# One of the first mixer's four weight sums made as a DRAM table, its column tiles paired across halves

## The chip, the cores and the metric

The kernel runs on one core of one Trainium2 chip. The metric is the device time of one execution in microseconds (us): the median of three runs, with the lowest and the highest beside it. A profile of one execution lies beside the runs; its numbers (span, busy times, waits, the start of an instruction) belong to that execution.

## The reference

Sequence length S = 2048, width D = 1024, hidden width F = 3584, bf16 in and out, batch 1. A linear attention block with a residual is followed by a mixer along the sequence with a residual:

```python
def _A_ref(x, wqkv, wo):
    qkv = (lambda x, *d: x.transpose(*d))((x @ wqkv).reshape(B, S, 3, H, Dh), 2, 0, 3, 1, 4)
    q, k, v = qkv[0], qkv[1], qkv[2]
    phi = lambda t: jnp.where(t > 0, t + 1, jnp.exp(t)) + 1e-6
    pq, pk = phi(q), phi(k)
    kv = jnp.einsum("bhsd,bhse->bhde", pk, v)
    ...
    return (lambda x, *d: x.transpose(*d))(o, 0, 2, 1, 3).reshape(B, S, D) @ wo
def _B_ref(x, w1, b1, w2, b2):
    h = _layernorm(x, axis=-1)
    u = jnp.einsum("bsd,sf->bdf", h, w1) + b1
    u = _gelu(u)
    y = jnp.einsum("bdf,fs->bds", u, w2) + b2
    return (lambda x, *d: x.transpose(*d))(y, 0, 2, 1)
x = A_x
h = x + _A_ref(_layernorm(x, axis=-1), A_wqkv, A_wo)
h2 = h + _B_ref(_layernorm(h, axis=-1), B_w1, B_b1, B_w2, B_b2)
```

The first mixer (`Mixer1`) is the product of w1, transposed, with the normalized h: F rows by D columns, summed over S. The second (`Mixer2`) multiplies with w2 and goes back to S rows.

## The kernel before

**Stages.** By the profile's times: layernorm of x and the products for k, v and q up to about 160 us; the output projection, with the residual and the two layernorms behind it folded into one, from about 168 to 225 us; the first mixer from 225 to 382 us; the second to the end.

**Products with seven multiplications.** Nearly all products use Strassen's scheme in Winograd's form: the operands are cut into two by two blocks, and seven products of sums of blocks replace eight. The stationary operand's blocks are called a11, a12, a21, a22, and its four sums are numbered by the product that they serve: sum 5 is a21 + a22, sum 6 is sum 5 - a11, sum 7 is a11 - a21, sum 3 is a12 - sum 6. In the first mixer the two halves of the contraction are the even and the odd row tiles of w1 (tiles of 128 rows), and the two halves of the output rows are two neighbouring column tiles of w1: tiles 2p and 2p + 1 for product p.

**Quads.** Two such products form a quad, which reads one w1 tile of 512 columns (`load_w1(u, part)`, in two or four parts). Four of the seven multiplications of the two (numbers 1, 5, 2 and 3) are done in common, once more by the seven-fold scheme (`Inner`: seven times four matmuls of 256 columns), the other three (4, 6, 7) as 48 matmuls of 512 columns in the gaps. `Quad.asums(m)` makes sum m for both products of a quad in one DVE instruction of 128x2048 elements, in a tile of the pool `sa`, which has four buffers for the first mixer and hands them out in turn. There are seven quads, and so seven such instructions per sum. The first quad's sums are made ahead of time, during the output projection, by the generator `first_sums` (line 1772).

**The output loop** (lines 1823 to 1864) runs over the 16 row tiles i in an order of its own. For each it holds, in program order: PE's matmuls (`out_mm`), the denominators of the attention (`den`), the mean of tile i - 1 on DVE (`h_mean`), the normalization of tile i - 3 on DVE, the evacuation on ACT (`out_evac`), the variance of tile i - 2 by a squaring on ACT (`h_var`, which needs that tile's mean), the scaling of the queries on DVE (`scale_q`), the spreading of the reciprocals to the partitions by SP's transfers (`den_spread`), and at i = 1, 2, 3, 5 and 6 the next step of `first_sums`. For the first nine tiles the residual x is added by an accumulating transfer that POOL issues (line 1716); for the others it is copied to the accumulator before the matmuls (`seed`), from tiles that SP loads.

**Order.** `pin` keeps an instruction in program order among the pinned ones of its engine or queue; the names `hv`, `ht`, `hs` and `hd` pin everything on DVE, PE, ACT and SP. In the output loop nearly everything is pinned. Waits for data are put in by the framework, for DRAM tiles too. A queue such as SP's issues in order: a transfer that has to wait holds up those behind it.

**The first stage.** Row tiles of x are normalized in turn (`ln_stats`, `ln_finish`) and transposed by a DMA that SP issues (line 980), each followed on SP by the load of a later row tile; `x_sums` on DVE reads the transposed tiles. The loop over q (line 1462) runs a `KRun` and a `VRun` for each pair of row tiles.

**What the steps touch.** `load_w1` (147), `load_w2` (163), `Product7.__init__` (327), `Mixer1` (434: the view of the w1 tile, the bias column `ft`), `Mixer2` (469), `Quad.asums` (604), `Quad.run_first` (756), `Quad.run1` with `starting` (798), the loop over q (1462), `out_evac` (1701) and `first_sums` (1772).

Of the kernel before, what the change touches and what calls it, by code (L numbers as in the profile page):

```python
# [10 lines left out]
P = 128  # L11
F32 = mybir.dt.float32
BF16 = mybir.dt.bfloat16
FP16 = mybir.dt.float16
ACT = mybir.ActivationFunctionType
ALU = mybir.AluOpType
# [18 lines left out]
def kernel(  # L35
# [12 lines left out]
    nc = tc.nc  # L48
    x = A_x.flatten_outer_dims()
    o_dram = out.flatten_outer_dims()  # L50
    S, D = x.shape
    F = B_w1.shape[1]
# [94 lines left out]
    def load_w1(u, part, hold=lambda ins: ins, parts=2):  # L147
        if part == 0:
            w1_tiles[u] = w_tile(wpool, WLEN)[:, 0:NS * CW].rearrange("p (k f) -> p k f", f=CW)
        k = slice(part * NS // parts, (part + 1) * NS // parts)  # L150
        hold(nc.sync.dma_start(
            w1_tiles[u][:, k, :],
            B_w1[:, u * CW:(u + 1) * CW].rearrange("(k p) f -> p k f", p=P)[:, k, :],
        ))

    WH = NFP * 2 * P
# [6 lines left out]
    def load_w2(p, second, q=nc.sync, ks=slice(0, NFP)):  # L163
        q.dma_start(
            (odd[p] if second else even[p % 2])[:, ks, :],
            B_w2[:, p * 2 * P:(p + 1) * 2 * P].rearrange("(k two p) s -> p k two s", two=2, p=P)[:, ks, second, :],
        )

    spans = (slice(0, NFP // 2), slice(NFP // 2, NFP))

# [28 lines left out]
        for part in phi_parts(dst, src, n, pool):  # L199
            part()  # L200

    dram = ctx.enter_context(tc.tile_pool(name="dram", bufs=1, space=bass.MemoryType.DRAM))
    sactx = ctx.enter_context(ExitStack())
    mctx = ctx.enter_context(ExitStack())

# [4 lines left out]
    hmov = {}  # L210
# [113 lines left out]
    class Product7:  # L324
        first = 0

        def __init__(self, p, w, nk, mov):
            self.p, self.nk, self.mov = p, nk, mov
            (self.a11, self.a21), (self.a12, self.a22) = [[v[:, :, h * P:(h + 1) * P] for h in range(2)] for v in w]
            self.lhs = {1: self.a11, 2: self.a12, 4: self.a22}  # L330

        def prefetch(self):
# [101 lines left out]
    class Mixer1(Product7):  # L434
        first = NSP // 4

        def __init__(self, p):
            c = (p % 2) * 2 * P
            w = w1_tiles[p // 2][:, :, c:c + 2 * P].rearrange("p (k two) f -> p k two f", two=2)
            super().__init__(p, (w[:, :, 0, :], w[:, :, 1, :]), NSP, hmov)  # L440

        def evac(self, fh, dh, ps, a=0, b=CW):
            ft = 2 * self.p + fh
            act.activation(
                (gE if fh == 0 else gO)[:, self.p, dh * CW + a:dh * CW + b],
                ps[:, a:b], ACT.Gelu_apprx_tanh, bias=b1_sb[:, ft:ft + 1], scale=1.0,
            )
# [20 lines left out]

    class Mixer2(Product7):
        def __init__(self, p):  # L470
            super().__init__(p, (even[p % 2], odd[p]), NFP, gmov)
            self.hr = {}

        def asum(self, m, home=None):
# [57 lines left out]
    class Quad:  # L532
# [71 lines left out]
        def asums(self, m):  # L604
            if not isinstance(self.sts[0], Mixer1):
                for st in self.sts:
                    st.asum(m)
                return
            v = w1_tiles[self.sts[0].p // 2].rearrange("p (k two) (s h f) -> p k two s h f", two=2, s=2, h=2)
            a11, a12, a21, a22 = (v[:, :, k, :, h, :] for h in range(2) for k in range(2))  # L610
            a, b, op = {
                5: (a21, a22, ALU.add),
                6: (self.S.get(5), a11, ALU.subtract),
                7: (a11, a21, ALU.subtract),
                3: (a12, self.S.get(6), ALU.subtract),
            }[m]
            t = self.S[m] = pools["sa"].tile([P, NSP, 2, P], FP16, tag="sa", name="sa")[:]
            for s, st in enumerate(self.sts):
                st.lhs[m] = t[:, :, s, :]
            return dve.tensor_tensor(t, a, b, op)  # L620

        def inner(self, m):
            mov, sink, sink_sum = {
# [132 lines left out]
        def run_first(self, nxt, before_inner, before_second):  # L756
            sts = self.sts
            for st in sts:
                st.p1()
            share(sts)  # L760
            for st in sts:
                st.p2()
            before_inner(slice(0, 2))
            self.in5.mov = self.mov5
            self.interleave(self.in5, self.steps(*[st.p6 for st in sts]))
            before_inner(slice(2, 4))
            nxt.begin1()
            self.base3()
            for i, st in enumerate(sts):
                st.apart = 1  # L770
                st.p7()
                before_second(slice(2 * i, 2 * i + 2))
            sts[0].p3()
            sts[1].p3_mm()
            self.late.append(sts[1].p3_evac)
            return sts, nxt
# [21 lines left out]
        def run1(self, pend, nxt, on_p4, third_sums=None):  # L798
            sts = self.sts
            s4, s6, s7 = self.steps(*[st.p4 for st in pend]), self.steps(*[st.p6 for st in sts]), self.steps(*[st.p7_fill for st in sts])  # L800
            c6, c7 = 3 * len(s6) // 4, len(s7) // 2

            def starting():
                self.in1.sums(slice(2, 4))
                self.asums(5)
                self.in5 = Inner(sts, 5, self.mov5, "i5", self.sink5, self.sum5)
                self.in5.sums(slice(0, 2))
                self.asums(6)
                self.t1 = self.base("t1a")
                for s, st in enumerate(sts):  # L810
                    st.begin(self.t1[:, s, :])

            def gelu(s, dh, t):
                return lambda: sts[s].evac(0, dh, t[:, s, :])

            def before_gelu():
                if third_sums is not None:
                    third_sums(slice(3, 4))
                gelu(0, 0, self.t1)()

            def gelu_late(*args):
                return lambda: self.late.insert(0, gelu(*args))

            self.in1.behind = self.late
            self.interleave(
                self.in1, s4, {"b": starting, "7": lambda: self.in5.sums(slice(2, 4))}, (("b", None), ("7", None))
            )
            self.asums(7)
            in2 = Inner2(sts, 2, self.mov2, "i1", self.add_to(self.t1), None)
            in2.sums()  # L830
            on_p4()
            nxt = nxt()
            share(sts)
            if third_sums is not None:
                third_sums(slice(0, 3))
            self.interleave(self.in5, s6[:c6], flush=(("b", None), ("7", None), ("end", None)), first=1)
            sts[0].finish()
            self.asums(3)
            self.base3()
            in3 = Inner2(sts, 3, self.mov3, "i5", self.add_to(self.t3), None)  # L840
            in3.sums()
            sts[0].with_shared(sts[0].base3, sts[0].B)
            self.interleave(
                in2, s6[c6:] + s7[:c7], {"third": before_gelu, "end": gelu_late(1, 0, self.t1)}, (("7", None),)
            )
            sts[1].with_shared(sts[1].base3, sts[1].B)
            if nxt is not None:
                nxt.begin1()
            self.interleave(in3, s7[c7:], {
                "third": gelu(0, 1, self.t3), "end": gelu_late(1, 1, self.t3),  # L850
            }, (("b", 1), ("c", None)))
            return sts, nxt
# [13 lines left out]
    with ExitStack() as actx:  # L866
# [33 lines left out]
        with ExitStack() as a1:  # L900
# [561 lines left out]
            for q in range(2, NVP):  # L1462
# [6 lines left out]
                for n in runs:  # L1469
# [46 lines left out]
                            x_sums(q, slice(3, 4))  # L1516

                    run_step(n, prev, after6, after5, after7, after3=after3)
                    prev = n
            r1, r2 = (QRun(1, half, late_home, late_mov) for half in range(2))  # L1520
            nc.vector.memset(zz[:, :, 0:3 * HB], 0.0)
# [102 lines left out]
        with ExitStack() as a3:  # L1624
# [73 lines left out]
            def rows(i):  # L1698
                return slice(order[i] * P, (order[i] + 1) * P)

            def out_evac(i, dcs=range(NDC)):
# [6 lines left out]
                for dc in dcs:  # L1708
                    cols = slice(dc * CW, (dc + 1) * CW)
                    out_ps = ps.pop((i, dc))  # L1710
                    if i in BY_ACT:
                        hs.activation(h_bfs[i][:, cols], out_ps[:], ACT.Copy, accum_out=row_sums[i][dc][:])
                    else:
                        hs.copy(h_bfs[i][:, cols], out_ps[:])
                    if i < SEEDED:
                        nc.gpsimd.dma_start(h_bfs[i][:, cols], x[rows(i), cols], accum_op=ALU.add)  # L1716
                    else:
                        hv.bn_stats(row_sums[i][:, dc, :], out_ps[:])
                if i >= SEEDED:
# [51 lines left out]

            def first_sums():
                cur = Quad([Mixer1(0), Mixer1(1)])
                for m in (5, 6, 7, 3):
                    yield pin(cur.asums(m))
                cur.in5 = Inner(cur.sts, 5, None, "i5", cur.sink5, cur.sum5)
                Held.on = True
                cur.in5.sums()
                Held.on = False
                yield cur  # L1780
# [326 lines left out]
```

## Time and profile before

| | us |
|---|---|
| median of 3 runs | 550.14 |
| lowest, highest | 549.45, 550.32 |
| the profiled execution | 550.33 |
| its span, first to last instruction | 548.5 |
| DVE sums of 128x2048 in the mixer, mean | 1.22 |
| w1 load of 512 KB, median to landing, 168 to 210 us | 6.3 |
| w1 load of 1024 KB, median to landing | 6.9 |
| spread of 128 KB (`shared_sb<-rd_dram`), median to landing, 168 to 200 us | 5.3 |
| transpose of x (`xnT<-xn`), median to landing | 3.1 |

The profiled execution took 0.2 us more than the median of the runs. Its span is what the profiler's views count from; 1.8 us lie around it. PE's granted clock is 0.999 throughout. Busy shares are given per engine; a matmul's listed duration overlaps that of the next, so PE's real pace is seen from the distance of starts. A timeline row has the start in us, the length of the run of alike instructions, engine, line, operation, what it writes and reads, how many, and in brackets how long the engine was idle before it and what ended that.

### The profile page before, as it was taken

The page shows a single profiled execution, that of the slowest core. Times are in us where ns is not written, and L with a number is a line of the kernel's source. Part 1 is how long each engine was busy: PE and PEld are TensorE (multiplying, and loading weights), DVE is VectorE, ACT ScalarE, POOL GpSimd, SP SyncE. Part 2 cuts the span into 40 slices and gives each one's busy share as a digit, 9 for nine tenths or more (in the row PEclk, how much of TensorE's full clock was granted, in tenths as well). Part 3 has the DMA queues.
Part 4 walks back from the last instruction along what each step waited for, and adds up shares of the span by engine and source line. Part 5 has one row for each costly group of instructions (what it writes and reads, how often), then busy time and mean ns, then how long its engine had stood idle before and what let it go on. Part 6 is the DMA issues. An engine that isn't in the chain of part 4 may idle for free.

```text
span 548.5 us, 10234 instructions
## 1 busy us (share of the span) xinstructions
PE 540.7 (99%) x3962; PEld 331.6 (60%) x3978; DVE 460.0 (84%) x889; ACT 290.9 (53%) x628; POOL 42.0 (8%) x54
## 2 busy tenths in 40 slices
PE   7999999999999999999999999999999999999997
PEld 3444446646864444456666766666455667877865
DVE  7798897867778577989988889888899899979877
ACT  5748777777687779645556465564220412312320
POOL 1000000000002350000000000000002103103111
PEclk9999999999999999999999999999999999999999
DMA  8933532200558999204041350513597759399344
GB/s 287 326 80 76 79 77 41 40 1 17 139 165 182 214 288 324 96 2 154 1 154 53 101 155 1 154 55 81 148 307 200 202 134 241 63 302 224 80 124 74
DMA packets 84513, 74.61 MB, mean 136 GB/s; under 512 B 16098, under 2 KB 77040, under 8 KB 84464
## 3 DMA queue, kind: packets, MB, share of 16 engines
q1 hardware_dynamic: 77344, 67.46, 42.7%
q0 software_dynamic: 6688, 6.04, 7.8%
q8 instruction: 31, 0.51, 0.4%
q10 hardware_dynamic: 432, 0.44, 0.2%
q14 instruction: 18, 0.15, 0.1%
HBM read 59.12 MB, written 11.67 MB: 129 GB/s over the span
## 4 chain that ended last, share of the span: by engine, by line
PE 87%; DMA 3%; DVE 3%; issue 3%; ACT 2%; POOL 1%; SPq 0%; POOLq 0%; ACTq 0%
PE psI L237 29%; PE psC L237 18%; PE psB L237 8%; PE psC L1068 4%; PE psB L1068 4%; PE psA L1068 4%; PE psA L237 3%; PE acc_t L984 3%; PE acc_t L237 2%; PE psE L1068 2%; PE psA L1202 2%; PE psC L1202 2%; PE psB L1202 2%; DMA wkv<-in_A_wqkv_dram 2%; DVE hst L237 1%
## 5 line engine op out<-in xcount | busy, mean ns | idle before, releaser
L237 PEld LDWEIGHTS <-is 128*128 128x128 f16 x820 | 80.2, 98 | 31.3 <-DVE is L237 0.2
L237 PEld LDWEIGHTS <-wq 128*128 128x128 bf16 (+1 forms) x610 | 59.6, 98 | 39.3 <-issue 1.9
L237 PEld LDWEIGHTS <-sa 128*128 128x128 f16 x571 | 55.8, 98 | 20.8
L237 PE MATMUL acc_t<-wo_sb,pqT 128*128 128x512 f16 x256 | 55.9, 380 | 0.0
L510 POOL DMA_DIRECT2D out_dram<-wq x28 | 24.4, 946 | 308.0 <-DMA wq<-in_B_w_dram 188.0
L237 PEld LDWEIGHTS <-pqT 128*128 128x128 bf16 x256 | 24.8, 98 | 30.6 <-issue 1.1
L237 PE MATMUL psC<-gs,wq 128*128 128x512 f16 x168 | 40.8, 379 | 0.0
L1068 PEld LDWEIGHTS <-xs 128*128 128x128 f16 x208 | 20.0, 98 | 22.2
L237 PE MATMUL psC<-hT,sa 128*128 128x512 f16 x112 | 31.2, 379 | 0.0
L1716 POOL DMA_DIRECT2D h_bf<-in_A_x_dram x18 | 15.8, 985 | 186.3 <-DVE pqT L237 170.0
L237 PE MATMUL psI<-hi,is 128*128 128x256 f16 x200 | 30.0, 273 | 0.0
L237 PE MATMUL psB<-hT,sa 128*128 128x512 f16 x112 | 29.7, 379 | 0.0
L237 DVE TENSOR_TENSOR t<-psI,t 128x256 f32<-128x256 f32 (+1 forms) x45 | 20.8, 475 | 9.4 <-PE psI L237 7.9
L237 PE MATMUL psC<-hT,wq 128*128 128x512 f16 x112 | 28.4, 379 | 0.0
L237 PE MATMUL psI<-gi,is 128*128 128x256 f16 x210 | 27.8, 273 | 0.0
L1068 PE MATMUL psA<-wkv,xnT 128*128 128x512 bf16 x96 | 25.6, 379 | 0.4
L1068 PEld LDWEIGHTS <-xnT 128*128 128x128 bf16 x156 | 15.2, 98 | 17.9 <-issue 0.2
L237 ACT COPY psI<-psI 128x256 f32<-128x256 f32 x50 | 18.0, 360 | 11.6 <-PE psI L237 9.8
L190 DVE TENSOR_SCALAR e_sb<-e_sb 128x512 bf16<-128x512 bf16 x64 | 18.2, 284 | 6.5 <-ACT e_sb L185 6.4
L984 PE MATMUL acc_t<-wkv,xnT 128*128 128x512 bf16 x94 | 21.9, 379 | 1.0 <-DMA wkv<-in_A_wqkv_dram 0.8
L237 DVE TENSOR_TENSOR sa<-wq 128x2048 f16<-128x2048 bf16 (+1 forms) x17 | 20.0, 1178 | 2.6 <-DMA wq<-in_B_w_dram 2.6
L953 DVE BATCH_NORM_STATS2 st<-x_sb 128x6 f32<-128x512 bf16 x32 | 20.6, 682 | 1.2 <-DMA x_sb<-in_A_x_dram 1.2
(265 smaller groups left out, 1139.5 us busy)
## 6 DMA issues: line engine op xcount, KB each, us to landing
wq<-in_B_w_dram SPq DMA_DIRECT2D x10, 1024.0 KB, 6.9
wq<-in_B_w_dram SPq DMA_DIRECT2D x20, 448.0 KB, 6.7
gs<-parked SPq DMA_DIRECT2D x9, 896.0 KB, 4.8
shared_sb<-rd_dram SPq DMA_DIRECT2D x32, 128.0 KB, 5.1
wq<-in_B_w_dram SPq DMA_DIRECT2D x8, 512.0 KB, 6.2
out_dram<-h_bf SPq DMA_DIRECT2D x16, 256.0 KB, 4.7
x_sb<-in_A_x_dram SPq DMA_DIRECT2D x14, 256.0 KB, 4.2
w2o<-in_B_w_dram SPq DMA_DIRECT2D x4, 896.0 KB, 10.1
```

The lines of the kernel that those rows point to most:

```text
L190: pin(nc.vector.tensor_scalar(e_sb[:], e_sb[:], 1.0, PHI_EPS, ALU.min, ALU.add))
L237: return (lambda *a, **kw: pin(op(*a, **kw))) if self.always or getattr(Held, self.key) else op
L510: nc.gpsimd.dma_start(to, ot[:, a:b], accum_op=ALU.add)
L953: return nc.vector.bn_stats(st[:, c, :], x_sb[:, c * CW:(c + 1) * CW])
L984: mm = nc.tensor.matmul(pp[:, 0:CW], lhsT=xnT[:, kt, i * P:(i + 1) * P], rhs=wkv[:, kt, c * CW:(c + 1) * CW], start=(kt == 0), stop=(kt == ...
L1068: pin(nc.tensor.matmul(ps[:], lhsT=lhs[:, k, :], rhs=rhs[:, k, :], start=(start and k == 0), stop=(k == hk2 - 1), skip_group_check=True,))
L1202: pin(nc.tensor.matmul(out[:, j], lhsT=rhs[:, k, 2 * self.half + j, :], rhs=lhs[:, k], start=(start and j == 0 and k == 0), stop=(k == hk2 ...
L1716: nc.gpsimd.dma_start(h_bfs[i][:, cols], x[rows(i), cols], accum_op=ALU.add)
```

## The change

Three things are changed together.

The column tiles of a product are paired across the two halves of F: product p has column tiles p and p + 14 (`NFP` is 14) instead of 2p and 2p + 1. A w1 tile then consists of two blocks of 256 columns, one from each half, and each load brings one of them; the bias column and the order of w2's rows follow. Sum 5 of all products is then the sum of the even and the odd row tiles over one contiguous half of w1's columns.

That sum is made once, as a table in DRAM (`s5_dram`, 1024 x 1792 in fp16): POOL issues a transfer that copies the even row tiles' half, converted, and one that adds the odd row tiles' half to it (`make_s5`). A store of two elements from SP stands before them, at a place in the loop over q. The accumulating transfers of the output loop are pinned.

The DVE instruction for sum 5 is replaced by a load of 128 x 2048 elements from the table by SP (`fetch5`), in `first_sums` for the first quad, and for the others one quad ahead, in `run_first` and `run1`.

```diff
     def load_w1(u, part, hold=lambda ins: ins, parts=2):
...
-        k = slice(part * NS // parts, (part + 1) * NS // parts)
+        k, h = slice(part // 2 * 2 * NS // parts, (part // 2 + 1) * 2 * NS // parts), part % 2
         hold(nc.sync.dma_start(
-            w1_tiles[u][:, k, :],
-            B_w1[:, u * CW:(u + 1) * CW].rearrange("(k p) f -> p k f", p=P)[:, k, :],
+            w1_tiles[u][:, k, h * 2 * P:(h + 1) * 2 * P],
+            B_w1.rearrange("(k p) (h f) -> p k h f", p=P, h=2)[:, k, h, u * 2 * P:(u + 1) * 2 * P],
         ))
...
-            B_w2[:, p * 2 * P:(p + 1) * 2 * P].rearrange("(k two p) s -> p k two s", two=2, p=P)[:, ks, second, :],
+            B_w2[:, p * 2 * P:(p + 1) * 2 * P].rearrange("(two k p) s -> p k two s", two=2, p=P)[:, ks, second, :],
         )
+
+    dram = ctx.enter_context(tc.tile_pool(name="dram", bufs=1, space=bass.MemoryType.DRAM))
+    s5_dram = dram.tile([NSP * P, F // 2], FP16, name="s5_dram")
+
+    def make_s5(held):
+        v = B_w1.rearrange("(k two p) (h f) -> k two p h f", two=2, p=P, h=2)
+        t = s5_dram.rearrange("(k p) f -> k p f", p=P)
+        pin(nc.sync.dma_start(s5_dram[0:1, 0:held.shape[-1]], held))
+        for two, op in ((0, ALU.bypass), (1, ALU.add)):
+            pin(nc.gpsimd.dma_start(t, v[:, two, :, 1, :], accum_op=op))
+
+    def load_s5(t, u):
+        return nc.sync.dma_start(t.rearrange("p k s f -> p k (s f)"), s5_dram.rearrange("(k p) f -> p k f", p=P)[:, :, u * 2 * P:(u + 1) * 2 * P])
...
-            c = (p % 2) * 2 * P
-            w = w1_tiles[p // 2][:, :, c:c + 2 * P].rearrange("p (k two) f -> p k two f", two=2)
-            super().__init__(p, (w[:, :, 0, :], w[:, :, 1, :]), NSP, hmov)
+            w = w1_tiles[p // 2].rearrange("p (k two) (h s f) -> p k two h s f", two=2, h=2, s=2)
+            super().__init__(p, [[w[:, :, k, h, p % 2, :] for h in range(2)] for k in range(2)], NSP, hmov)
...
-            ft = 2 * self.p + fh
+            ft = self.p + NFP * fh
...
+            return dve.tensor_tensor(self.sa_tile(m), a, b, op)
+
+        def sa_tile(self, m):
             t = self.S[m] = pools["sa"].tile([P, NSP, 2, P], FP16, tag="sa", name="sa")[:]
             for s, st in enumerate(self.sts):
                 st.lhs[m] = t[:, :, s, :]
-            return dve.tensor_tensor(t, a, b, op)
+            return t
+
+        def fetch5(self):
+            return load_s5(self.sa_tile(5), self.sts[0].p // 2)
...
             before_inner(slice(2, 4))
             nxt.begin1()
+            nxt.fetch5()
             self.base3()
...
                 self.in1.sums(slice(2, 4))
-                self.asums(5)
                 self.in5 = Inner(sts, 5, self.mov5, "i5", self.sink5, self.sum5)
...
             sts[0].finish()
+            if nxt is not None:
+                nxt.fetch5()
             self.asums(3)
...
                     run_step(n, prev, after6, after5, after7, after3=after3)
+                    if kind == "K" and q == 2:
+                        make_s5(xnT[0:1, 0, 0:2].bitcast(FP16))
                     prev = n
...
-                        nc.gpsimd.dma_start(h_bfs[i][:, cols], x[rows(i), cols], accum_op=ALU.add)
+                        pin(nc.gpsimd.dma_start(h_bfs[i][:, cols], x[rows(i), cols], accum_op=ALU.add))
...
                 cur = Quad([Mixer1(0), Mixer1(1)])
-                for m in (5, 6, 7, 3):
+                yield pin(cur.fetch5())
+                for m in (6, 7, 3):
                     yield pin(cur.asums(m))
```

## The prediction

> **What bounds the kernel now.** I read the page first, then the busy time by stage, then the chain that ended last, then the timelines of the engines around the changed steps.
>
> ```profile
> span 548.5 us, 10234 instructions
> ...
> PE 540.7 (99%) x3962; PEld 331.6 (60%) x3978; DVE 460.0 (84%) x889; ACT 290.9 (53%) x628; POOL 42.0 (8%) x54
> ...
> q1 hardware_dynamic: 77344, 67.46, 42.7%
> q0 software_dynamic: 6688, 6.04, 7.8%
> ```
>
> A busy PE need not be a PE at its peak, so I checked its rate. In the first mixer the chain shows 8 matmuls of 256 columns in 0.87 us and 5 of 512 columns in 1.08 us: 0.109 and 0.216 us each. One quad has 4 inner products of 28 short matmuls and 48 long ones: 112 x 0.109 + 48 x 0.216 = 22.6 us. The quads start at 264.03, 286.67 and 309.30 us, a period of 22.63. PE does nothing but issue there, and the sums that the change takes from DVE are hidden behind it. In the whole stretch from 180 to 385 us PE waits once, for 0.4 us. What can be won is a few tenths of a microsecond; the question is what the change can break.
>
> ```profile
> 182.00:196.00 14.00, 14.00 (x72) 6.08 (x71) 6.82 (x11) 9.70 (x26) 5.29 (x7) 1.00 1.04 243
> ...
> 322.00:336.00 14.00, 14.00 (x103) 9.91 (x102) 11.24 (x25) 7.07 (x16) 0.00 (x0) 1.00 0.47 150
> ```
>
> The columns are the stretch, its length, then busy us of PE, weight loads, DVE, ACT and POOL, the granted clock, DMA share and GB/s. In the first row, the output projection, the DMA engines are full (1.04); in a quad, even while w1 arrives, half idle.
>
> ```profile
> 197.81 7.13 DMA h_bf<-in_A_x_dram
> ...
> 212.14 1.31 DVE hst L237 x2
> ...
> 229.10 0.50 ACT psB L237
> 229.60 0.04 issue
> 229.64 2.53 PE psA L237 x11
> ```
>
> These are pieces (start, length) of the chain that ended last. From 186 to 229.6 us it does not run through PE: it goes from the POOL-issued residual transfers through ACT and DVE to the first mixer's matmuls. PE is full beside it, but only 0.4 us stand between the two, so a delay of this chain is paid.
>
> **Part 1, the sum removed.** Seven DVE sums of 128x2048 at 1.22 us (8.5 us) go. Six lie in quads where PE never waits, the first at 176.60 us where DVE has idle time on both sides. Worth 0.
>
> **Part 2, column tiles paired across halves.** w1 comes in 512-byte rows instead of 1024. In the stretch 294 to 308 us, w1 traffic takes 46.7% x 16 x 14 us / 2.10 MB = 50 engine-us per MB; from 350 to 372 us, with 512-byte w2 rows, 25.6% x 16 x 22 / 1.62 = 56. So 12% more: a pair of loads lands in 7.4 us instead of 6.6. It is issued at 252.8 us, so at 260.2, and is first read by DVE at 265.65. Covered by 5 us; without that cover 0.8 us per quad, 5 us in all. Views of sums, bias column and w2 row order move without another instruction: 0.
>
> **Part 3, the table.** A tiny store on SP follows the load at 49.59 us; then POOL issues two transfers of 3.67 MB, the second after the first has landed. No row shows DRAM to DRAM. The page gives 42.7% x 16 x 548.5 / 67.46 = 56 engine-us per MB for plain traffic and 7.8% x 16 x 548.5 / 6.04 = 113 for accumulating. The plain one lies between 204 and 415 engine-us, the accumulating one at 415. On 16 engines the two last 39 to 52 us; if only half the engines serve them, 77 to 104. They start near 52 us and end between 91 and 156. POOL's next transfer starts at 172.88 us and the first fetch at 184.7, so even the slow end has 17 us to spare: 0, up to the first rival below.
>
> The Trainium skill (DMA: Bandwidth & Descriptors, "Why a DMA increments its semaphore by 16 and not by 1") says that the engines of one transfer are the largest number up to 16 that divides the slowest dimension of both sides. Here that dimension is k = 8, so by it 8 engines would serve the table, the 77 to 104 us above; on 16 the sum is the same, as both lie under cover.
>
> **Part 4, the six fetches inside the mixer.** 512 KB each. The fetch for the next quad follows the end of the inner product that reads the old buffer (258.8 us), behind w1 until 260.2; adding 6.3 us, the landing of a 512 KB w1 quarter in the busy stretch 168 to 210 us, gives 266.5 at worst, and DVE needs it at 270.95. Cover 4 us: 0. The third sum of quad 1 now waits for that same end, which came at 258.8 against its start at 259.00: 0.
>
> **Part 5, the first fetch.** This is the step that is not covered. The sum was made on DVE at 176.60, and the next sum, which reads it, at 180.39:
>
> ```profile
> 176.60 1.22 DVE L620 TENSOR_TENSOR sa<-wq 128x2048 f16<-128x2048 bf16 x1
> ...
> 179.24 1.23 DVE L237 TENSOR_TENSOR pqT<-pqT,shared_sb 128x2048 bf16<-128x2048 bf16 x1 [1.16 <-DMA shared_sb<-rd_dram]
> 180.39 1.22 DVE L620 TENSOR_TENSOR sa<-sa,wq 128x2048 f16<-128x2048 f16 x1
> 181.52 0.15 DVE L237 TENSOR_TENSOR hsum<-hsum,hsum 128x1 f32<-128x1 f32 x1
> ```
>
> The fetch takes its place at i=1 of the output loop, but on SP's queue, which is in program order, and there it stands behind the reciprocals' store and eight spreads:
>
> ```profile
> 178.03 0.34 SPq L237 DMA_DIRECT2D rd_dram<-shared_sb  x1
> 180.94 3.70 SPq L237 DMA_DIRECT2D shared_sb<-rd_dram  x8
> 184.93 0.36 SPq L237 DMA_DIRECT2D out_dram<-h_bf  x1
> ```
>
> So it is issued at 184.7, after the moment at which DVE wants it. Landing bounds: 5.3 us (median of the spreads from 168 to 200 us) to 9.2 us (the longest wq load in the mixers' stretch 240 to 400 us). It stands behind 1 MB of spreads in a full stage, so I take 7.2 us, the longest landing of a spread: L = 191.9. DVE stands from 180.4 to 191.9, and what is queued behind is the mean of row tile 2, for which ACT waits:
>
> ```profile
> 189.39 1.15 ACT L237 ACTIVATE squares<-h_bf,mv_all 128x1024 bf16<-128x1024 bf16 x1
> ...
> 191.10 1.05 ACT L237 CAST h_bf<-acc_t 128x512 bf16<-128x512 f32 x2
> 194.56 1.15 ACT L237 ACTIVATE squares<-h_bf,mv_all 128x1024 bf16<-128x1024 bf16 x1 [2.41 <-DMA h_bf<-in_A_x_dram]
> ```
>
> After L come the sum (1.15) and the mean (0.5), so the square starts at L + 1.65. The two casts start 1.71 later and take 1.05, so the next square starts at L + 4.41 = 196.3 instead of 194.56. ACT's old wait of 2.41 us absorbs the rest. The delay is L - 190.15 = 1.75 us; it shifts the evacuation of tile 6, POOL's transfer for it (197.23), its landing (204.94) and with it the chain to 229.64. DVE's own backlog (8.6 us of work, done at 200.5 instead of 194.0) is cut by its idle times of 2.4, 0.6, 1.0, 1.0 and 0.6 us up to 212, which leaves 1.0; so ACT decides. PE's tile 8 would wait some 0.4 us for its scaled operand, inside the same delay. Bounds: L = 190.0 gives 0; L = 193.9 gives 3.75.
>
> **Sum.** 0 + 0 + 0 + 0 + 1.75: the profiled execution, 550.33 us with its span of 548.5, becomes 552.1; from the median of the runs, 550.14, **551.9**.
>
> **Rivals.** (a) *No slower.* The first fetch lands by 190.15, that is 5.45 us after issue. For it: spreads and stores in this stretch land in a median of 5.3 and 5.8 us. Against: it is four times a spread's bytes and behind eight of them. ACT's slack then covers all, and the time stays at 550.1; the 0.4 us wait at 229.6 is all that could be won. It decides up to L = 191.2 (1.1 us).
>
> (b) *The table slows the transposes.* From 52 us on, its transfers share the engines with the DMA transposes of x, which must land before DVE's sums:
>
> ```profile
> 73.70 1.24 SPq L980 DMA_TRANSPOSE xnT<-xn  x1
> ...
> 79.76 0.41 DVE L1057 TENSOR_TENSOR xs<-xnT 128x512 f16<-128x512 bf16 x1
> ```
>
> Landing takes 3.1 us, so 3.0 us are left here and 4.0 at the pair before (60.38 to 67.47). If a shared engine only halves its rate, a transpose takes up to 6.2 and nothing happens. But a transpose moves in small packets: the stretch 50 to 80 us, with four of them, has 4950 under 512 bytes, some 77 per transpose and engine. If each waits for one table row, it is dear: a row of 3.6 KB at 56 to 113 engine-us per MB is 0.2 to 0.4 us, so 15 to 31 us per transpose. Less the slack, two late deadlines cost 23 to 55 us: 573 to 605. Against it: in the output projection POOL's and SP's transfers already share engines, and loads still land in 6 us.
>
> The Trainium skill (DMA: Bandwidth & Descriptors, "Queues, rings and completion order") has each engine alternate between queues by packets of several descriptors, not by single ones. By its figure of 9 to 17 descriptors a packet the wait is an estimated 5 to 9 rows per transpose, 1 to 3.5 us, mostly inside the slack. No row here shows a transpose beside POOL traffic.
>
> (c) *The table is late.* If DRAM to DRAM runs at half the accumulating rate on 8 engines, the two last 208 us and end at 260: SP, POOL and DVE stand, about 75 us, 625. Against: a margin of 17 us at the slowest row.
>
> (d) *Faster by over 1.1 us.* PE would have to do its matmuls faster; nothing removed is PE's.
>
> **How the numbers follow.** The forecast (1.1 to 4 us, so 551.2 to 554.1) has 0.52, (a) 0.30, (b) 0.11, (c) 0.04, (d) 0.03. A measurement tells 0.2%, 1.1 us, from no change. So slower 0.67, same 0.30, faster 0.03. The range runs from 549.9, under rival (a), to 558, which takes in the upper bound of the first fetch and a transpose or two some microseconds late; left out are (b) in full, (c) and (d). The forecast's own range is 551.2 to 554.1.
>
> **What would show it.** Right: the second sum on DVE starts after 190 us, with an idle time of some 10 us before it put down to the fetch; ACT's square of tile 2 waits for DVE; the wait before 229.6 us grows by about 1.8 us; the quads keep 22.63 us. Wrong: DVE's sums of x waiting on transposes before 110 us (b), SP standing before the first fetch (c), or a fetch that lands before 190 (a). A quad longer than 22.63 us would refute parts 2 and 4.

## The result, and the profile after

The changed kernel takes 592.59 us (median of 4 runs, 591.25 to 593.36) against 550.23 us before (549.45 to 551.55): a ratio of 1.0765, 95% interval 1.0734 to 1.0795. The forecast was 551.9 us, the range 549.9 to 558. The page of the changed kernel:

```profile
span 589.5 us, 10252 instructions
...
PE 548.6 (93%) x3978; PEld 332.8 (56%) x3978; DVE 452.2 (77%) x882; ACT 291.7 (49%) x628; POOL 45.2 (8%) x56
...
q1 hardware_dynamic: 98962, 71.13, 48.1%
q0 software_dynamic: 10816, 13.40, 12.2%
```

DVE has 8 us less to do, as planned, POOL's queue 7.4 MB more, and PE, full before, now stands. The busy time by stage shows where (stretch, length, busy us of PE, weight loads, DVE, ACT, POOL, granted clock, DMA share, GB/s):

```profile
56.00:70.00 14.00, 10.21 (x159) 4.57 (x160) 6.14 (x15) 3.80 (x8) 1.93 (x1) 0.77 0.98 154
70.00:84.00 14.00, 5.57 (x26) 2.35 (x24) 5.54 (x11) 5.91 (x12) 0.00 (x0) 0.84 1.17 110
84.00:98.00 14.00, 5.30 (x12) 1.64 (x12) 0.00 (x0) 1.17 (x2) 0.00 (x0) 0.55 1.09 121
98.00:112.00 14.00, 4.36 (x15) 1.71 (x16) 4.90 (x12) 1.68 (x4) 0.00 (x0) 0.63 0.87 99
```

The counts tell more than the busy times: 12 and 15 matmuls in 14 us, with DVE and ACT all but idle from 84 to 98 us. The DMA share lies around 1 and above it at only 100 to 150 GB/s. It does not say that the engines are full: it adds up the times of the packets of both queues, and a packet's time can hold waiting. From 70 to 84 us SP's queue has 68.4% for 627 packets, 0.24 us each; from 50 to 80 us before the change it was 49.0% for 5590, 0.04 us each. The prediction's "full (1.04)" has the same limit. The chain that ended last (start, length, what) names what was waited for:

```profile
47.70 15.87 DMA xnT<-xn
...
69.89 36.79 DMA xnT<-xn
```

Two transposes of x took 15.9 and 36.8 us from their issue to their landing; before, the median was 3.1. POOL's and SP's timelines put the table's transfers beside them:

```profile
39.27 1.09 POOL L177 DMA_DIRECT2D s_dram<-in_B_w_dram  x1 [36.37 <-DMA s_dram<-xnT]
62.98 1.93 POOL L177 DMA_DIRECT2D s_dram<-in_B_w_dram  x1 [22.61 <-DMA s_dram<-in_B_w_dram]
```

```profile
43.47 1.26 SPq L999 DMA_TRANSPOSE xnT<-xn  x1
...
47.70 9.29 SPq L999 DMA_TRANSPOSE xnT<-xn  x1
57.04 0.57 SPq L959 DMA_DIRECT2D x_sb<-in_A_x_dram  x1
66.04 1.64 SPq L999 DMA_TRANSPOSE xnT<-xn  x1
...
69.89 18.98 SPq L999 DMA_TRANSPOSE xnT<-xn  x1
88.92 2.76 SPq L959 DMA_DIRECT2D x_sb<-in_A_x_dram  x1
```

The copy lasts from 39.3 to 62.9 us, the accumulating transfer from 63.0 to 106.1 (landings 23.4 and 43.1 us after issue). Two transposes and a load of x fall under each (the transposes issued at 43.47 and 47.70, and at 66.04 and 69.89), and all four land late, after 15.0, 15.9, 25.3 and 36.8 us. The second of each pair lands just behind the transfer that it lay under: at 63.6 against 62.7, and at 106.7 against 106.1. Even their issue, 1.24 us before, holds SP up for 9.3 and 19.0 us. DVE's timeline shows who pays:

```profile
52.94 0.69 DVE L1158 TENSOR_TENSOR vaug<-psC,e 128x512 bf16<-128x512 f32 x1
63.59 0.43 DVE L1076 TENSOR_TENSOR xs<-xnT 128x512 f16<-128x512 bf16 x1 [9.95 <-DMA xnT<-xn]
...
106.70 0.43 DVE L1076 TENSOR_TENSOR xs<-xnT 128x512 f16<-128x512 bf16 x1 [30.33 <-DMA xnT<-xn]
```

Two waits of 9.95 and 30.33 us, 40.3 in all. POOL's first residual transfer of the output loop starts at 212.66 instead of 172.88: 39.8 of the 41.0 us of span are lost by then. The remaining 1.2 are the first fetch (SP, then DVE, then ACT):

```profile
220.80 3.63 SPq L249 DMA_DIRECT2D shared_sb<-rd_dram  x8
224.63 0.38 SPq L180 DMA_DIRECT2D sa<-s_dram  x1
```

```profile
231.05 1.23 DVE L628 TENSOR_TENSOR sa<-sa,wq 128x2048 f16<-128x2048 f16 x1 [11.01 <-DMA sa<-s_dram]
```

```profile
232.58 1.15 ACT L249 ACTIVATE squares<-h_bf,mv_all 128x1024 bf16<-128x1024 bf16 x1 [3.29 <-DVE mv_all L249]
...
235.77 1.15 ACT L249 ACTIVATE squares<-h_bf,mv_all 128x1024 bf16<-128x1024 bf16 x1 [0.43 <-DMA h_bf<-in_A_x_dram]
```

Behind the spreads, an idle time of 11.0 us on DVE, ACT's square waiting 3.3 us for the mean, and of its old 2.41 us of slack 0.43 left. In the mixer nothing changed: PE waits for no engine between 272 and 420 us, and quads start at 305.37 and 328.00 us, 22.63 apart.

### The profile page after: what moved, and what is told of

The parts are those of the page before. It is cut to its first block, busy times and chain, and to the rows that moved or that the text cites. A ratio compares the mean times of both kernels' runs of the same rounds, so it can differ in the third digit from the quotient of the medians.

```text
span 589.5 us, 10252 instructions
## 1 busy us (share of the span) xinstructions
PE 548.6 (93%) x3978; PEld 332.8 (56%) x3978; DVE 452.2 (77%) x882; ACT 291.7 (49%) x628; POOL 45.2 (8%) x56
## 3 DMA queue, kind: packets, MB, share of 16 engines
q0 software_dynamic: 10816, 13.40, 12.2%
## 4 chain that ended last, share of the span: by engine, by line
PE 79%; DMA 12%; DVE 3%; issue 3%; ACT 1%; POOL 1%; ACTq 0%; POOLq 0%; SPq 0%; DVEq 0%
PE psI L249 27%; PE psC L249 16%; DMA xnT<-xn 9%; PE psB L249 8%; PE psB L1087 3%; PE psA L1087 3%; PE acc_t L1003 3%; PE psC L1087 3%; PE psA L249 3%; PE acc_t L249 2%; PE psA L1221 2%; PE psC L1221 2%; PE psB L1221 2%; PE psE L1087 1%; DVE hst L249 1%
## 5 line engine op out<-in xcount | busy, mean ns | idle before, releaser
L249 PEld LDWEIGHTS <-wq 128*128 128x128 bf16 (+1 forms) x610 | 59.7, 98 | 39.8 <-issue 2.5
L1087 PE MATMUL psA<-wkv,xnT 128*128 128x512 bf16 x104 | 28.9, 404 | 21.5 <-DMA xnT<-xn 21.5
L1087 PEld LDWEIGHTS <-xnT 128*128 128x128 bf16 x156 | 15.9, 103 | 42.3 <-DMA xnT<-xn 22.5
L1076 DVE TENSOR_TENSOR xs<-xnT 128x512 f16<-128x512 bf16 x14 | 5.8, 415 | 40.3 <-DMA xnT<-xn 40.3
L1100 ACT COPY psB<-psA 128x512 f32<-128x512 f32 x19 | 10.9, 573 | 33.2 <-PE psA L1087 26.4
```

The lines of the kernel that those rows point to most:

```text
L249: return (lambda *a, **kw: pin(op(*a, **kw))) if self.always or getattr(Held, self.key) else op
L1076: pin(nc.vector.tensor_tensor(out, a, b, op))
L1087: pin(nc.tensor.matmul(ps[:], lhsT=lhs[:, k, :], rhs=rhs[:, k, :], start=(start and k == 0), stop=(k == hk2 - 1), skip_group_check=True,))
L1100: pin(nc.scalar.copy(self.B[:], self.A[:]))
```

## The experiments

My theory after the result (theory 1 below): a transfer that shares a DMA engine with the table's rows is served between them and lands late by the length of the rows that pass it; all of the 40 us come from the two transposes that DVE waits for. Rivals: the table having only half of the engines (2), a share of time or bytes regardless of the rows (3), traffic from DRAM to DRAM as such, and the accumulation. Of e1, e4, e6, e7 and e8 there is one time each; 23 runs of the kernel before lie between 549.1 and 551.45 us.

### More engines, the same place (e1_sixteen)

```diff
-        v = B_w1.rearrange("(k two p) (h f) -> k two p h f", two=2, p=P, h=2)
-        t = s5_dram.rearrange("(k p) f -> k p f", p=P)
+        v = B_w1.rearrange("(k two p) (h f) -> two p k h f", two=2, p=P, h=2)
+        t = s5_dram.rearrange("(k p) f -> p k f", p=P)
...
-            pin(nc.gpsimd.dma_start(t, v[:, two, :, 1, :], accum_op=op))
+            pin(nc.gpsimd.dma_start(t, v[two, :, :, 1, :], accum_op=op))
```

> The table's two transfers are addressed with the 128 rows of a tile as the slowest dimension instead of the 8 tiles; place, bytes and rows are those of the changed kernel. Theory 1 (a transpose's small packets take turns with table rows on every engine that both use): the transfers last half as long, some 12 and 20 us instead of 23.6 and 43, so they end near 74 us instead of 106; the transposes that fall under them still land late, and 10 to 20 of the 40 us remain: 560 to 575 us. Theory 2 (the loss comes from the table having only half the engines, which become the slow half of every other transfer): with all 16 engines nothing stays behind, under 5 us remain: 550 to 556 us. If the transfers last as long as before, the number of engines was not 8.

Measured: 565.26 us. The transfers land after 14.1 and 23.6 us instead of 23.4 and 43.1. DVE's wait for transposes, in the list of waits (us in total, times, longest):

```profile
DVE xs L1076 <- DMA xnT<-xn: 12.8, 2, 10.7
```

Theory 1's range. Theory 2 is out: with all engines in use the transposes still take up to 20.0 us. That the other order of dimensions nearly halves the transfers agrees with the Trainium skill (DMA: Bandwidth & Descriptors, "Why a DMA increments its semaphore by 16 and not by 1"), whose rule gives 8 engines to the one and 16 to the other. No view here counts the engines themselves, but where the table's copy has the queues to itself, from 112 to 124 us, its queue's share of the 16 engines' time is 56.7% in e6 (addressed as in the changed kernel) and 104.2% in e2 (as here).

### The table after the last transpose (e2_late16)

```diff
-                    if kind == "K" and q == 2:
-                        make_s5(xnT[0:1, 0, 0:2].bitcast(FP16))
+                    if kind == "Q" and q == 5 and n.half == 1:
+                        make_s5(xnT[0:1, 0, (NS - 1) * P:(NS - 1) * P + 2].bitcast(FP16))
```

> As e1, and the table is started only after the last transpose of x (row tile 15) has landed, near 109 us. Theory 1: no transpose meets the table, so the 40 us go altogether; the table ends near 145 us, before the spreads that start at 150.7. What remains is the wait of DVE for the first fetch, which the blind reading of the changed kernel's profile puts at 1.25 us: 551 to 552.5 us. A rival, that the loss has to do with the traffic itself (any transfer from DRAM to DRAM beside the matmuls) and not with the transposes, gives a loss of the size of the transfers' length, over 20 us: above 570 us.

Measured: 551.30 us, ratio 1.0021, interval 1.0010 to 1.0031. The table starts at 110.8 us, transposes land in 3.0 to 4.7 us, and the 40 us are gone. The traffic is all there, so it is not that. The table ended at 151.1 us and not near 145, so the first spreads were issued 4.7 us behind their store instead of 1.7; POOL's first residual transfer was not later for it (172.68 us). 1.2 us remain.

### The pairing alone (e3_pair)

`make_s5` and the fetches are taken out, and sum 5 is made by DVE where it was:

```diff
-                yield pin(cur.fetch5())
-                for m in (6, 7, 3):
+                for m in (5, 6, 7, 3):
...
                 self.in1.sums(slice(2, 4))
+                self.asums(5)
```

> The pairing of the column tiles alone: no table, no fetch, sum 5 on DVE as before. Prediction of parts 1 and 2: nothing, 549.5 to 550.9 us, and quads of 22.63 us with w1 loads that land some 0.8 us later. If the 512-byte rows matter, up to 5 us more.

Measured: 550.18 us, ratio 0.9998, interval 0.9989 to 1.0006. A w1 pair lands in 7.5 us in the stretch 249 to 272 us, where it took 6.6; nobody waits for it.

### Short rows (e4_small)

```diff
         for two, op in ((0, ALU.bypass), (1, ALU.add)):
-            pin(nc.gpsimd.dma_start(t, v[:, two, :, 1, :], accum_op=op))
+            for c in range(7):
+                f = slice(c * 2 * P, (c + 1) * 2 * P)
+                pin(nc.gpsimd.dma_start(t[:, :, f], v[:, two, :, 1, f], accum_op=op))
```

> The changed kernel with each table transfer cut into seven of 256 columns, so that a row is 512 bytes instead of 3584; the same bytes, the same 8 engines, the same place. Theory 1 (taking turns row by row, packet by packet): each packet of a transpose waits for some 50 ns instead of 160 to 290, a transpose lands in 6 to 8 us instead of 15 to 37, and under 12 of the 40 us remain: below 562 us. Theory 3 (a transpose gets a share of the engine's time or bytes, or nothing until the table transfer is over): the loss stays near 40 us as long as the table takes as long: 580 us and more.

Measured: 570.20 us, between the two theories. Transposes land in 9.5 us (median) and 12.9 at most: shorter rows do let them through, but less than in proportion to the row, and the table lasts as long (its last transfer is issued at 89.6 us and lands after 18.9), so a third deadline is missed:

```profile
DVE xs L1078 <- DMA xnT<-xn: 15.7, 3, 6.5
```

The run changes more than the row. The pages count 35584 packets in POOL's queue here and 21248 in e8, the same rows on 16 engines: 14336 more, one for each row, all under 512 bytes (10816 and 8768, so 2048, for the changed kernel and e1). And the queue's share goes up to 140.6% of 16 engines (56 to 61 us), where the changed kernel's is 48.2% from 70 to 84 us; so the transfers, several in flight at once, were most likely not held to the same 8 engines. e8 is the cleaner run for the row's length.

### The fetch ahead of the spreads (e5_early_fetch)

e2 with one step of `first_sums` moved:

```diff
             load_w1(0, 3, pin, 4)
+            next(ahead)
             scale_q(2, 0, 1)
...
-            den_at, sums_at = {1: 1, 3: 0}, (1, 2, 3, 5, 6)
+            den_at, sums_at = {1: 1, 3: 0}, (2, 3, 5, 6)
```

> e2 with the first fetch put earlier on SP's queue: behind the last quarter of the first w1 tile, ahead of the spreads (issued near 165 instead of 184.8 us). If the 1.2 us that e2 lost are DVE's wait for that fetch, they go: 549.6 to 550.6 us, no idle time of DVE before the second sum, ACT's square of tile 2 not waiting for DVE. If they are the fetch's traffic in the full stage or the pinned POOL transfers, the time stays at 551 to 551.6.

Measured: 550.08 us, ratio 1.0000, interval 0.9991 to 1.0009. The fetch is issued at 166.2 us, and DVE's second sum and ACT's squares are back where they were:

```profile
180.96 1.22 DVE L628 TENSOR_TENSOR sa<-sa,wq 128x2048 f16<-128x2048 f16 x1
```

```profile
189.73 1.14 ACT L249 ACTIVATE squares<-h_bf,mv_all 128x1024 bf16<-128x1024 bf16 x1
...
194.93 1.15 ACT L249 ACTIVATE squares<-h_bf,mv_all 128x1024 bf16<-128x1024 bf16 x1 [2.44 <-DMA h_bf<-in_A_x_dram]
```

So the 1.2 us of e2 are DVE's wait for the fetch, and the change with both defects removed is worth nothing: 8.5 us of DVE work less, the same time.

### Late, on 8 engines (e6_late8)

e2's place with the changed kernel's addressing.

> e2 with the table on 8 engines again, as in the changed kernel: it starts near 111 us, and its second transfer runs from 134 to 173 us or later, under the spreads at 150 to 157, the first w1 tile at 160 to 165 and up to POOL's residual transfers at 172.7. Theory 1 (whatever shares an engine with table rows lands late): spreads and w1 land in 10 to 30 us instead of 5 to 6, DVE waits for them, and the time is 556 to 575 us. Rival (only transposes suffer, with their packets of 256 bytes): 551 to 553 us.

Measured: 570.14 us. No transpose is late (4.7 us at most); now the denominators' reciprocals are. SP's timeline and the list of waits:

```profile
150.23 0.34 SPq L249 DMA_DIRECT2D rd_dram<-shared_sb  x1
168.47 3.63 SPq L249 DMA_DIRECT2D shared_sb<-rd_dram  x8
```

```profile
ACT shared_sb L249 <- DMA rd_dram<-shared_sb: 11.6, 1, 11.6
...
DVE pqT L249 <- DMA shared_sb<-rd_dram: 7.2, 2, 5.4
```

Before, SP's spreads followed their store after 1.7 us (150.73, 152.46); here after 18.2. Transposes are not special: a store of 128 KB suffers too, and the spreads behind it land after 11.2 us (median) instead of 4.5. The loads of w1 did not land late as expected (6.9 us): they were issued only at 178 us, and the table was over at 180.1.

### Two copies (e7_copies)

```diff
-        for two, op in ((0, ALU.bypass), (1, ALU.add)):
+        for two, op in ((0, ALU.bypass), (1, ALU.bypass)):
```

> The changed kernel with the second table transfer a plain copy too; the addition in the table is left out. Theory 1 (the length of a table row on its engine counts): both transfers last 23.6 us, the table ends near 87 us instead of 106, the first wait of DVE stays at 10 us and the second falls from 30 to some 11: 570 to 576 us. Rival (the accumulating transfer is what holds the others up): the second wait goes, 560 to 564 us. If the bytes alone counted, the time would stay at 592.

Measured: 574.81 us. The longest landing of a transpose falls from 36.8 to 19.1 us:

```profile
DVE xs L1076 <- DMA xnT<-xn: 22.8, 2, 12.5
```

As expected from the row's time on its engine: a copy holds transposes up too, and accumulation counts by making each row slower (the two transfers land after 23 to 25 us each).

### Short rows on 16 engines (e8_small16)

> 16 engines as in e1 and 512-byte rows as in e4, at the early place. e1 left 15 us of the 40 and e4 20. If the two act on different factors (how long the table shares the engines; how long a packet waits for a row), some 40 x 15/40 x 20/40 = 7.5 us remain: 555 to 560 us. If both act on one thing, the time is not below e1's 565.

Measured: 564.02 us, against 555 to 560: missed. The first two pairs of transposes still take 10.4 to 11.9 us, about as in e4. The two measures don't multiply, and the table lasts longer than with long rows: to 88.1 us instead of 77.5 in e1.

The traces let the packets of the two queues be counted, and in e1 and here, with the table on 16 engines, the count is one for one while both are at work. In e1, with rows of 3584 bytes, POOL's queue has 641 packets and SP's 640 from 63 to 75 us; here, with rows of 512 bytes, 2271 and 2269 from 66 to 78 us. That is theory 1's turn by turn, whatever the row's length, and neither a share of the bytes nor a wait for the table's end. Two costs were missing from the expectation. After a transpose is issued none of its packets moves for some 4 us in either run (e1, 58 to 62 us: 227 packets of POOL's queue, 1 of SP's; here, 60 to 65 us: 1757 and none); before the change they move after about 1 us. And a packet with its 512-byte row takes 0.085 us on an engine (12 us x 16 / 2269), where the rows alone pass in 0.028 (2501 from 44.6 to 49 us). Why either is so stays open.

## Why the prediction was wrong

**The step that failed is part 3, "the table: 0".** I asked whether the table would be ready in time, not what it would do to others while it is made. The runs showed in its place that the rows of the table go turn by turn with the packets of the transposes of x, so that DVE waited 40.3 us for two transposes. The table's own length I had somewhat too long: 77 to 104 us on 8 engines were forecast, 66.5 measured (23.4 + 43.1). Its start I had too late: SP issued the two-element store at 36.96 us, not behind the load at 49.59. By the kernel's text the loads and transposes of that stage are not pinned, so they need not hold a pinned store back; no run tests this.

**Rival (b) was right in mechanism and price, and wrong in its chance.** It named the transposes, each packet of which waits for a row, two late deadlines, and 573 to 605 us; 592.6 was measured. Only one of its two pairs was late: it meant those with DVE's sums at 67.47 and 79.76 us of the kernel before, and late were those of 54.15 and 67.47, as the table started at 39.3 us and not near 52. I gave it 0.11, for two reasons that both fell. The first: that loads already share engines with POOL's transfers in the output projection and land in 6 us. But those are transfers of 128 KB, 8 rows of 1 KB per engine, soon past; the table is 128 rows of 3.6 KB per engine, one behind the other for 23 and 43 us. The second: that an engine which halves its rate only doubles a landing. A transpose's landing grew by 12 to 34 us; it is many small packets, and long rows go between them.

Beside them stood my estimate from the Trainium skill (DMA: Bandwidth & Descriptors, "Queues, rings and completion order"), whose turns of 9 to 17 descriptors I used for the transpose's side alone. I let the table take one row per turn, which gave 1 to 3.5 us per transpose; the section sets no smaller turn for one queue than for another, and turns of one size on both sides come to one row per packet of the profile (which counts each row of the table, and each 256 bytes of a transpose, as one), the price of rival (b). Measured were 12.8 and 33.7 us more on 8 engines (15.9 and 36.8 against 3.1). One row per packet fits that: 136 packets per engine lie in the two transposes and the load that SP issued from 66.0 to 69.9 us (2 x 64 of 256 bytes and 8 of 2 KB, if they spread over 16 engines), and they were through at 106.7, 0.30 us per packet, near the 0.34 us that a row of the accumulating transfer took (43.1 us over 128). The counts of e1 and e8 show the one for one directly; the 4 us at the start and the pace with short rows are not explained by it.

**Part 5 held in all but size.** DVE's wait was 11.0 us where I had 11.5; shifted back by the 39.8 us, the fetch was there at 191.3 against my 191.9. The cost was 1.2 us against 1.75, and the prediction's own sum with L = 191.3 gives 1.15. e2 shows it alone and e5 removes it.

**Parts 1, 2 and 4 held.** The removed sums are worth 0 (e5 has them removed at ratio 1.0000), the pairing 0 (e3; 7.5 us for a w1 pair against 7.4 forecast), and the fetches inside the mixer land in 4.0 us, well inside their cover. The reading that PE's pace leaves nothing to win was right too: rival (d) never appeared.

## What to carry to other kernels

A bulk transfer that is "hidden" costs what it does to the others on its engines: list every transfer with a deadline that will be in flight beside it, above all those of many small packets, and count their packets times its row, not bytes, up to the time that the bulk transfer is in flight. Put it where nothing with a deadline is in flight, and give it all the engines, so that it is over sooner; the second alone recovered 27 of the 42 us, both together 41. And a load that replaces an instruction is issued from its queue's place in the order, not from the instruction's: here eight spreads stood before it.

## What was not expected of the hardware

- Issuing can stall: SP took 9.3 and 19.0 us to issue a transpose that takes 1.24 otherwise, while the table's transfers ran. Everything behind it on SP's queue started as much later. With rows of 512 bytes it was 4.3 us at most (e8).
- Two queues at work on the same 16 engines moved equal numbers of packets, whatever their length: 641 rows of 3584 bytes and 640 packets of 256 in 12 us of e1, 2271 of 512 bytes and 2269 in 12 us of e8.
- The accumulating DRAM-to-DRAM transfer took 43.1 us for the bytes that the converting copy moved in 23.4 (8 engines), and 23.6 against 14.1 on 16.
- The granted clock fell to between 0.55 and 0.84 in the stretches where PE stood, and was back at 1.00 from 112 us on. With the late table on 16 engines it stayed at 1.00.
